# A stack copy moved to VectorE, register loads among the products, and w1 in smaller pieces

## The chip, the cores and the metric

The kernel runs on one core of one Trainium2 chip. The time is the device time of one execution in microseconds; with several executions it is their median. TensorE is called PE in the profile, VectorE DVE, ScalarE ACT, GpSimd POOL and SyncE SP.

## The reference

Two stages, one behind the other, in float32.

1. Local attention. Inputs `q`, `k`, `v` are 4 x 8 heads x 768 rows x 64. Each chunk of 32 rows attends to 8 memory rows, 16 rows on its left, its own 32 and 8 on its right, 64 columns in all: `softmax(q k^T / 8) v`.
2. A mixture of experts. The 3072 tokens of 512 numbers each choose one of 8 experts by the largest of 8 logits. An expert keeps up to `capacity` (768) tokens. It computes `relu(x w1) w2` with `w1` 512 x 1024 and `w2` 1024 x 512, and the result is weighted with the gate's probability and put back at the token's row; all other rows are zero.

How many tokens an expert has depends on the data, so the kernel reads the counts into registers and branches on them.

## The kernel before, in words

**Precision.** A product of two float32 matrices is made from three matmuls on split operands: each operand is a rounded part (`hi`) and the rest (`lo`), and `hi*hi + lo*hi + hi*lo` is summed in PSUM. So each weight matrix has to be split before use: ACT casts `hi` from the raw weights, and DVE or POOL subtracts to get `lo` (`split` for `w1`, `split2` for `w2`).

**Attention.** 24 tiles of 128 tokens, `t` = 0 to 23, run as a pipeline written out by hand: in step `t` come the scores of tile `t` (L502), the transposes of the tile before, the value product of the one before that (`value`, L539), the transposes of its output and the logits. SP loads `k` and `q` two segments ahead and `v` in blocks of two tiles. DVE copies the overlapping value rows (`copy_v`, L407, instructions of L417). Once a group of tiles has its logits, `route` gives small DVE operations, one at each `tick`, that compute expert and slot of each token; POOL then scatters the rows to DRAM (`put`, L799). In the steps of `W1_AT` SP also loads a quarter of expert 0's `w1` (L226), and in the steps of `PLAN` an eighth of it is split: the cast on ACT (L826), the subtraction on POOL (L827).

**Expert 0 ahead of the rest.** The first 256 rows of expert 0 (`EARLY`) are computed while the last tokens are still routed: `early` does their first layer, and `expert(0)` their second, in two products of 24 matmuls each, of 128 rows, `mm2` with t = 0 and 1. Each is read out by DVE as `y` (L959, `put_y`) and scattered by POOL (L960).

**An expert.** `layer1` computes the first layer for 512 columns in four pairs of blocks. The number of columns that are really computed is chosen by `If` on the count `m` (256, 320, 384 or 512, a branch of L893). ACT and DVE turn each block into `hhi` and `hlo` (`relu`, L875 and L876), and between the pairs the next expert's `w2` is split. Then come the tiles of the second layer, the last tile first (`last_tile`, L927): eight blocks of two matmuls, with the transposes of the next expert's rows in between, in fours. Where the last tile holds at most 64 rows, its `hhi` and `hlo` are laid side by side in one tile, so that the third matmul of each block can be left out. That copy is `stack` (L920): it copies 64 columns of `hlo` into the free columns of `hhi`, for blocks 0 to 5 behind the third pair and for blocks 6 and 7 behind the fourth. It is POOL's, under a `Switch` on bit 1 of `m + 1`.

**What sets the order.** Each engine runs its own list in the order of the program text, with semaphores between engines. So a late instruction on POOL holds whoever needs its result, and all that stands behind it on POOL. All loads of SP share the DMA engines with POOL's scatters and with the loading of instructions.

**Registers.** `values` (L793) loads numbers of an SBUF tile into the registers of an engine (TENSOR_LOAD in the trace): `m` for PE, DVE and POOL, `a` (from the tile `big`) for these and ACT. Before the change this is done in `experts`, ahead of expert 0's second layer. The banks `p2` are `lgp`, `b0` and the four of `p1`; `p1` are the banks of the first layer.

## Time and profile before

| what | value |
|---|---|
| median of 3 runs | 501.32 us (500.46 to 507.27) |
| the profiled execution | 505.29 us, of which the span is 503.5 us |
| PE, DVE, ACT, POOL busy | 463.4, 310.7, 232.0, 119.6 us |
| DMA, mean over the span | 157 GB/s, 79.26 MB |
| granted PE clock, mean | 0.986 |

The span reaches from the first to the last instruction. Busy time counts an engine's computing instructions. Matmuls are pipelined and their ends are modelled, so two matmuls in a row overlap in the rows, and the step from start to start is what one costs. In a timeline, what stands in brackets is the idle time of the engine ahead of the row, and what is held to have ended it.

### The profile page before, as it was taken

The page shows a single profiled execution, that of the slowest core. Times are in us where ns is not written, and L with a number is a line of the kernel's source. Part 1 is how long each engine was busy: PE and PEld are TensorE (multiplying, and loading weights), DVE is VectorE, ACT ScalarE, POOL GpSimd, SP SyncE. Part 2 cuts the span into 40 slices and gives each one's busy share as a digit, 9 for nine tenths or more (in the row PEclk, how much of TensorE's full clock was granted, in tenths as well). Part 3 has the DMA queues.
Part 4 walks back from the last instruction along what each step waited for, and adds up shares of the span by engine and source line. Part 5 has one row for each costly group of instructions (what it writes and reads, how often), then busy time and mean ns, then how long its engine had stood idle before and what let it go on. Part 6 is the DMA issues. An engine that isn't in the chain of part 4 may idle for free. (4 is left out here: it accounts for less than half of the span.)

```text
span 503.5 us, 12006 instructions
## 1 busy us (share of the span) xinstructions
PE 463.4 (92%) x4317; PEld 390.1 (77%) x4317; DVE 310.7 (62%) x676; ACT 232.0 (46%) x415; POOL 119.6 (24%) x160
## 2 busy tenths in 40 slices
PE   7899989898889985998999999999999999799993
PEld 6778877676678784887777899889988988677782
DVE  5989798998767642556645635745552685575310
ACT  6588768688442321525434415624430563443300
POOL 7621133556535341020200210010022011010011
PEclk9899999999999998899999999999999999999998
DMA  8687698987674666036470472534501644540011
GB/s 210 140 211 164 164 251 230 239 216 203 173 252 180 172 261 213 5 105 214 173 259 12 169 272 76 189 122 161 171 29 49 236 170 159 180 153 29 3 40 42
DMA packets 79393, 79.26 MB, mean 157 GB/s; under 512 B 33330, under 2 KB 60078, under 8 KB 79216
## 3 DMA queue, kind: packets, MB, share of 16 engines
q1 hardware_dynamic: 74416, 62.33, 43.3%
q0 software_dynamic: 4800, 14.95, 7.8%
q8 instruction: 65, 1.06, 0.9%
q14 instruction: 112, 0.92, 0.6%
HBM read 61.25 MB, written 15.99 MB: 153 GB/s over the span
## 5 line engine op out<-in xcount | busy, mean ns | idle before, releaser
L875 ACT ACTIVATE hhi<-ps 128x512 fp32r<-128x512 f32 x68 | 40.7, 599 | 148.8 <-PE ps L862 136.7
L876 DVE SCALAR_TENSOR_TENSOR hlo<-ps,hhi 128x512 fp32r<-128x512 f32 x68 | 47.0, 691 | 72.5 <-ACT hhi L875 69.7
L960 POOL DMA_INDIRECT out_dram<-y,tok x28 | 31.8, 1137 | 196.6 <-DVE y L959 73.6
L953 PE MATMUL ps<-w2hi,hhi 128*128 128x512 f32 x160 | 64.1, 401 | 1.4 <-DVE hlo L344 1.4
L862 PE MATMUL ps<-xhi,w1hi 128*128 128x320 f32 (+3 forms) x288 | 59.4, 328 | 5.9 <-DVE hlo L876 2.2
L953 PE MATMUL ps<-w2lo,hhi 128*128 128x512 f32 x160 | 62.9, 393 | 0.0
L953 PE MATMUL ps<-w2hi,hlo 128*128 128x512 f32 x160 | 62.5, 391 | 0.0
L862 PE MATMUL ps<-xhi,w1lo 128*128 128x320 f32 (+3 forms) x288 | 57.7, 322 | 0.0
L862 PE MATMUL ps<-xlo,w1hi 128*128 128x320 f32 (+3 forms) x288 | 57.6, 322 | 0.0
L862 PEld LDWEIGHTS ps<-xhi,w1hi 128*128 128x128 f32 x288 | 45.2, 188 | 10.4 <-ACT w2hi L853 3.7
L862 PEld LDWEIGHTS ps<-xhi,w1lo 128*128 128x128 f32 x288 | 45.9, 188 | 3.0
L862 PEld LDWEIGHTS ps<-xlo,w1hi 128*128 128x128 f32 x288 | 45.9, 188 | 2.8
L959 DVE TENSOR_SCALAR y<-ps,xg 128x512 f32<-128x512 f32 x20 | 15.0, 750 | 49.8 <-PE ps L953 45.0
L854 DVE TENSOR_TENSOR w2lo<-raw,w2hi 128x512 fp32r<-128x512 f32 x64 | 42.5, 705 | 0.0
L843 DVE TENSOR_TENSOR xlo<-ps,xhi 128x512 fp32r<-128x512 f32 x34 | 23.4, 690 | 27.2 <-ACT xhi L842 26.6
L827 DVE TENSOR_TENSOR w1lo<-raw,w1hi 128x512 fp32r<-128x512 f32 x56 | 36.6, 684 | 2.6 <-DVEq L846 0.6
L842 ACT CAST xhi<-ps 128x512 fp32r<-128x512 f32 x34 | 19.9, 587 | 38.8 <-PE ps L838 32.0
L953 PEld LDWEIGHTS ps<-w2hi,hhi 128*128 128x128 f32 x160 | 30.0, 188 | 8.6 <-DVE hlo L344 1.6
L853 ACT CAST w2hi<-raw 128x512 fp32r<-128x512 f32 x64 | 36.3, 620 | 0.0
L552 PE MATMUL ps<-vw,pT 128*32 128x130 f32 x768 | 29.2, 277 | 7.3 <-issue 3.7
L826 ACT CAST w1hi<-raw 128x512 fp32r<-128x512 f32 x64 | 35.5, 620 | 0.8
L953 PEld LDWEIGHTS ps<-w2hi,hlo 128*128 128x128 f32 x160 | 30.1, 188 | 7.0
(163 smaller groups left out, 810.3 us busy)
## 6 DMA issues: line engine op xcount, KB each, us to landing
raw<-in_moe_w_dram SPq DMA_DIRECT2D x15, 2048.0 KB
raw<-in_q_dram SPq DMA_DIRECT2D x11, 512.0 KB
raw<-in_k_dram SPq DMA_DIRECT2D x10, 512.0 KB
vw<-in_v_dram SPq DMA_DIRECT2D x49, 64.0 KB
xg<-x_d SPq DMA_DIRECT2D x3, 792.0 KB
vw<-in_v_dram SPq DMA_DIRECT2D x31, 72.0 KB
xg<-x_d SPq DMA_DIRECT2D x4, 528.0 KB
xg<-x_d SPq DMA_DIRECT2D x2, 1056.0 KB
```

The costliest lines, as they stand in the source:

```text
L552: nc.tensor.matmul(ps[32 * c4:32 * c4 + 32, i * 130:i * 130 + 130], pT[:, pr * P + 32 * c4:pr * P + 32 * c4 + 32], vw[:, c + c4 + 1, :, pr ...
L826: self.nc.scalar.copy(out=hi[sl], in_=raw[sl])
L827: (eng or self.nc.vector).tensor_tensor(out=lo[sl], in0=raw[sl], in1=hi[sl].bitcast(F32), op=ALU.subtract)
L842: nc.scalar.copy(out=self.xhi[:, d:d + k, sl], in_=pv)
L843: nc.vector.tensor_tensor(out=self.xlo[:, d:d + k, sl], in0=pv, in1=self.xhi[:, d:d + k, sl].bitcast(F32), op=ALU.subtract)
L853: self.nc.scalar.copy(out=self.w2a[:, j], in_=self.raw2[:, j])
L854: self.nc.vector.tensor_tensor(out=self.w2b[j // 4][:, j % 4], in0=self.raw2[:, j], in1=self.w2a[:, j].bitcast(F32), op=ALU.subtract)
L862: self.nc.tensor.matmul(ps, a[:, d, fs], b[:, d, o:o + w], start=(i + d == 0), stop=(i == 2 and d == KD - 1))
L875: self.nc.scalar.activation(out=self.hhi[hs], in_=ps, func=AF.Relu)
L876: self.nc.vector.scalar_tensor_tensor(out=self.hlo[hs], in0=ps, scalar=0.0, in1=self.hhi[hs].bitcast(F32), op0=ALU.max, op1=ALU.subtract)
L953: self.nc.tensor.matmul(ps, a[:, f, t * P:t * P + P], b, start=(f == 0 and i == 0), stop=(f == KF - 1 and i == 2))
L960: nc.gpsimd.indirect_dma_start(out=self.out[:, :], out_offset=bass.IndirectOffsetOnAxis(ap=tok[:, t:t + 1], axis=0), in_=y, in_offset=None ...
```

## The change

Three edits.

1. `stack` runs on DVE, under an `If` of DVE alone on a register `mv` that only DVE loads; and it stands directly behind the relu, ahead of the two `split2` of its pair.
2. The loads of `m` and `a` move out of `experts` into `expert(0)`: `m` (and DVE's `mv`) between the two early products, `a` within the second. The two products go to `p2[0]` (`lgp`) and `p2[1]` (`b0`); before they went to `p2[1]` (`b0`) and `p2[2]` (the first bank of `p1`). The second product's `y` is made ahead of the transposes of the third and fourth quarter.
3. Expert 0's `w1` is loaded in eight parts of 256 KB in the steps 3, 5, ..., 17 (before: four of 512 KB in 11, 13, 15, 17) and split in sixteen parts of 128x256 in the steps 6 to 21 (before: eight of 128x512 in 14 to 21).

```diff
-W1_AT = (11, 13, 15, 17)
-PLAN = ((14, 6), (15, 6), (16, 6), (17, 6), (18, 6), (19, 6), (20, 6), (21, 6))
+W1_LOAD, W1_SPLIT = range(3, 19, 2), range(6, 22)
...
-            if t in W1_AT:
-                k = W1_AT.index(t)
-                nc.sync.dma_start(out=self.raw1[:, k, :], in_=self.w1[0, k * P:(k + 1) * P, :])
-            split1(t)
+            if t in W1_LOAD:
+                _, d, f = w1_part(W1_LOAD.index(t), len(W1_LOAD))
+                nc.sync.dma_start(out=self.raw1[:, d, f], in_=self.w1[0, d * P:(d + 1) * P, f])
+            if t in W1_SPLIT:
+                self.split(self.raw1, self.w1hi, self.w1lo, w1_part(W1_SPLIT.index(t), len(W1_SPLIT)), nc.gpsimd)
...
-        self.m = self.values(self.m32, ENGS, 4 * nt + 1)
-        self.a = self.values(self.big, ENGS + (ET.Activation,), 2)
...
+            if g >= KF - 4:
+                self.stack(e, slice(0, g + 2) if g == KF - 4 else slice(g, g + 2))
             for _ in fs:
                 if todo2:
                     self.split2(todo2)
-            if g >= KF - 4:
-                self.stack(e, slice(0, g + 2) if g == KF - 4 else slice(g, g + 2))
...
-        for n in self.tc.Switch({ET.Pool: ((self.m[e] + 1) >> 1) & 1}, 2):
-            if n:
-                self.nc.gpsimd.tensor_copy(out=self.hhi[:, fs, o + P // 2:o + P], in_=self.hlo[:, fs, o:o + P // 2])
+        with self.tc.If((self.mv[e] + 1) & 2):
+            self.nc.vector.tensor_copy(out=self.hhi[:, fs, o + P // 2:o + P], in_=self.hlo[:, fs, o:o + P // 2])
...
-            for t in range(TA - 1):
-                self.layer2(e, t, tok)
-            ps = self.p2[self.order.index(TA - 1)]
-            for i, fs in enumerate((range(0, 3), range(3, 6), range(6, KF))):
-                self.mm2(ps, TA - 1, fs)
-                self.trans_x(e, i, 1)
-            self.put_y(e, ps, TA - 1, tok)
-            self.trans_x(e, KD - 1, 1)
+            self.mm2(self.p2[0], 0, range(KF))
+            self.m = self.values(self.m32, ENGS, 4 * self.nt + 1)
+            self.mv = self.values(self.m32, ET.DVE, 4 * self.nt + 1)
+            self.put_y(e, self.p2[0], 0, tok)
+            self.mm2(self.p2[1], 1, range(0, 3))
+            self.trans_x(e, 0, 1)
+            self.mm2(self.p2[1], 1, range(3, 6))
+            self.trans_x(e, 1, 1)
+            self.a = self.values(self.big, ENGS + (ET.Activation,), 2)
+            self.mm2(self.p2[1], 1, range(6, KF))
+            self.put_y(e, self.p2[1], 1, tok)
+            for d in range(2, KD):
+                self.trans_x(e, d, 1)
```

**The stack copy in expert 0.** On POOL, before, behind the third pair of blocks (L1048 and L923 are the `Switch`: the register arithmetic, the computed branch and its hints):

```order
L1048 SWITCH_STRIDE
L1048 ISA
L1048 REGISTER_ALU
L1048 ISA x2
L923 BRANCH_PREFETCH_HINT
L1048 UNCONDITIONAL_BRANCH
L923 BRANCH_PREFETCH_HINT
L925 COPY hhi<-hlo 128x6x64
```

On DVE, now, at the same place (L872 are the two relus of the pair, L919 the `If`):

```order
L872 SCALAR_TENSOR_TENSOR hlo<-ps,hhi 128x512 x2
L919 REGISTER_ALU x2
L919 COMPARE_AND_BRANCH
L920 COPY hhi<-hlo 128x6x64
L919 UNCONDITIONAL_BRANCH x2
```

The copy has left POOL and stands between the relus of one pair and the branches of the next; in the other experts the two `w2` subtractions follow it.

**The first early product on PE.** Before (L342 ends the early first layer):

```order
L342 MATMUL ps<-xlo,w1hi 128x256 x8
L795 TENSOR_LOAD m_77
L795 TENSOR_LOAD big
L953 MATMUL ps<-w2hi,hhi 128x512
L953 MATMUL ps<-w2lo_2753,hhi 128x512
```

Now the first product (into `lgp`) follows L340, the former L342, at once, and the load of `m` stands at its end:

```order
L948 MATMUL lgp<-w2hi,hhi 128x512
L948 MATMUL lgp<-w2lo_3042,hhi 128x512
L948 MATMUL lgp<-w2hi,hlo 128x512
L791 TENSOR_LOAD m_77
L948 MATMUL ps<-w2hi,hhi 128x512
L948 MATMUL ps<-w2lo_2773,hhi 128x512
```

The loads no longer stand ahead of the first product; `big` is loaded after the second group of four transposes, inside the second product.

## Rows read from the trace of the kernel before

**Rows 1.** The page, part 1: busy time of each engine (share of the span) and instructions.

```profile
PE 463.4 (92%) x4317; PEld 390.1 (77%) x4317; DVE 310.7 (62%) x676; ACT 232.0 (46%) x415; POOL 119.6 (24%) x160
```

**Rows 2.** PE's waits: line, what it waited for, us in total, times, longest us.

```profile
PE lgp L932 <- POOL hhi L925: 6.2, 1, 6.2
...
PE ps L862 <- DVE w2lo L854: 2.0, 1, 2.0
```

**Rows 3.** Windows of 2 us in expert 0: window, its length, busy us (and instructions) of PE, PEld, DVE, ACT and POOL, granted clock, DMA share, GB/s.

```profile
194.00:196.00 2.00, 0.39 (x3) 0.19 (x2) 0.86 (x2) 0.60 (x1) 0.00 (x0) 1.00 1.02 359
196.00:198.00 2.00, 0.00 (x0) 0.00 (x0) 0.00 (x0) 0.00 (x0) 0.00 (x0) 1.00 1.02 379
198.00:200.00 2.00, 0.00 (x0) 0.00 (x0) 0.00 (x0) 0.00 (x0) 0.00 (x0) 0.72 0.28 111
200.00:202.00 2.00, 1.36 (x3) 1.16 (x4) 0.00 (x0) 0.00 (x0) 0.51 (x1) 0.50 0.01 4
```

**Rows 4.** Timeline at the last tile of expert 0: start, us, engine, line, operation, idle time ahead.

```profile
194.06 0.33 PE L871 MATMUL ps<-pad 128*64 128x64 f32 x2
...
200.08 0.51 POOL L925 CAST hhi<-hlo 128x384 fp32r<-128x384 f32 x1 [6.23 <-DMA raw<-in_moe_w_dram]
...
200.64 0.79 PE L932 MATMUL lgp<-w2hi,hhi 128*128 128x512 f32 x1 [6.25 <-POOL hhi L925]
...
205.74 0.48 PE L932 MATMUL lgp<-w2hi,hhi 128*128 128x512 f32 x1
```

**Rows 5.** The same place in expert 1, where the copy is not needed.

```profile
235.49 0.50 PE L932 MATMUL lgp<-w2hi,hhi 128*128 128x512 f32 x1
...
238.25 0.49 PE L932 MATMUL lgp<-w2hi,hhi 128*128 128x512 f32 x1
```

**Rows 6.** Sequencers: single instructions of the `Switch` on POOL in the window from 194 to 200 us (duration ns min/median/max, first and last start), and the branches of the width helper L893 on DVE and on PE over the whole span.

```profile
L1048 POOLq COMPARE_BRANCH  x1: 43/43/43, 194.5 to 194.5; - x1
...
L923 POOLq BRANCH_PREFETCH_HINT  x1: 43/43/43, 199.8 to 199.8; - x1
...
L893 PEldq COMPARE_BRANCH  x92: 64/207/3489, 176.9 to 463.7; - x92
L893 DVEq COMPARE_BRANCH  x92: 41/56/69, 180.3 to 469.1; - x92
```

**Rows 7.** Register loads of `values` on PE's sequencer, same columns.

```profile
L795 PEldq TENSOR_LOAD <-m x1: 781/781/781, 162.0 to 162.0; - x1
L795 PEldq TENSOR_LOAD <-big x1: 600/600/600, 162.9 to 162.9; - x1
```

**Rows 8.** Timeline at the first early product.

```profile
161.86 1.11 PE L342 MATMUL ps<-xlo,w1hi 128*128 128x256 f32 x8
...
164.33 0.50 PE L953 MATMUL ps<-w2hi,hhi 128*128 128x512 f32 x1 [1.36 <-DVE hlo L344]
...
166.06 2.48 DVE L854 TENSOR_TENSOR w2lo<-raw,w2hi 128x512 fp32r<-128x512 f32 x4
```

**Rows 9.** Timeline at the start of expert 0's first layer.

```profile
178.28 0.74 DVE L959 TENSOR_SCALAR y<-ps,xg 128x512 f32<-128x512 f32 x1
178.89 0.59 ACT L842 CAST xhi<-ps 128x512 fp32r<-128x512 f32 x1 [1.25 <-PE ps L871]
...
179.17 0.82 PE L862 MATMUL ps<-xhi,w1hi 128*128 128x320 f32 x4 [1.46 <-DVE y L959]
```

**Rows 10.** POOL's and DVE's timelines in the attention stage.

```profile
89.29 1.28 POOL L827 TENSOR_TENSOR w1lo<-raw,w1hi 128x512 fp32r<-128x512 f32 x1 [3.29 <-ACT w1hi L826]
...
93.72 1.27 POOL L827 TENSOR_TENSOR w1lo<-raw,w1hi 128x512 fp32r<-128x512 f32 x1 [1.64 <-ACT w1hi L826]
...
89.14 0.16 DVE L700 SCALAR_TENSOR_TENSOR r_slot<-r_idx,r_pos 128x4 f32<-128x4 f32 x1
89.33 1.25 DVE L703 SCALAR_TENSOR_TENSOR r_dst<-r_ov,r_slot 128x4 int32<-128x4 f32 x1
...
93.77 1.76 DVE L417 COPY vw<-vw 24x768 f32<-24x768 f32 x1
```

**Rows 11.** Scores of the tiles 3, 14 and 22 on DVE (the row maximum, one for each tile).

```profile
28.38 0.67 DVE L519 TENSOR_REDUCE m<-ps 128x8 f32<-128x512 f32 x1
...
84.16 0.68 DVE L519 TENSOR_REDUCE m<-ps 128x8 f32<-128x512 f32 x1
...
132.43 0.68 DVE L519 TENSOR_REDUCE m<-ps 128x8 f32<-128x512 f32 x1
```

**Rows 12.** Groups of instructions by shape: line, engine, operation, tiles, shape, count, busy us, mean ns of one.

```profile
L826 ACT CAST w1hi<-raw 128x512 fp32r<-128x512 f32 x64 | 35.5, 620 | 0.8
...
L925 POOL CAST hhi<-hlo 128x384 fp32r<-128x384 f32 x5 | 3.2, 632 | 59.3 <-ACT w2hi L853 53.1 <-DMA raw<-in_moe_w_dram 6.2
...
L925 POOL CAST hhi<-hlo 128x128 fp32r<-128x128 f32 x5 | 1.8, 355 | 23.2 <-PE ps L838 9.8 <-ACTq L912 5.0 <-DVE xlo L843 4.9
...
L325 ACT CAST xhi<-ps 128x256 fp32r<-128x256 f32 x4 | 1.2, 387 | 1.4 <-DMA raw<-in_moe_w_dram 1.4
...
L498 DVE COPY kw<-kw 64x672 f32<-64x672 f32 x9 | 4.6, 506 | 1.4 <-ACT kw L481 1.3
```

**Rows 13.** A window of 10 us in the attention stage (columns as in rows 3), and SP's loads of `w1` (duration of the issue, ns min/median/max).

```profile
30.00:40.00 10.00, 9.24 (x186) 7.55 (x185) 9.39 (x26) 8.22 (x14) 3.96 (x9) 1.00 1.01 230
...
L226 SPq DMA_DIRECT2D raw<-in_moe_w_dram x4: 449/542/1525, 78.3 to 114.2; - x4
```

More of the change, by code (lines that the diff above doesn't have):

```diff
@@ L184, in attention, with w1_part @@
         ends = {t0 + w - 1: g for g, (t0, w) in enumerate(GROUPS)}
-        todo = [(k, slice(f, f + F // 2)) for k in range(KD) for f in (0, F // 2)]
-        def split1(t):
-            if any(i == t for i, _ in PLAN):
-                self.split(self.raw1, self.w1hi, self.w1lo, (slice(None), *todo.pop(0)), nc.gpsimd)
+        def w1_part(i, n):
+            w = KD * F // n
+            return slice(None), i * w // F, slice(i * w % F, i * w % F + w)
         for t in range(NTL):
@@ L975, in expert @@
         tc, nc = self.tc, self.nc
-        m, a = self.m[e], self.a[e]
         todo1 = list(range(KF)) if e + 1 < E else []
@@ L994, in expert @@
             nc.sync.dma_start(out=self.raw2, in_=self.w2[e + 1].rearrange("(k p) d -> p k d", p=P))
+        m, a = self.m[e], self.a[e]
         def split1(n):
```

## The prediction

> **What bounds the kernel now.** I read the page first, then PE's waits, then the windows and timelines around the longest of them. TensorE is busy for 463.4 of the 503.5 us [rows 1], so the kernel is bound by it and what can be won is mostly its idle time. The reader is to see in the list of PE's waits that one wait alone holds 6.2 us: L932, the first matmul of the last tile, behind POOL's `hhi` copy of L925, once [rows 2]; two shorter ones (1.4 and 1.5 us) stand at the start of the early second-layer product and of the first layer [rows 8, 9]. The windows show what the long one costs beyond itself: from 196 to 200 us PE does nothing, and the granted clock is 0.72 from 198 and 0.50 from 200 [rows 3].
>
> The timeline of that place [rows 4]: PE issues its last small matmul at 194.06 (0.33 long), and starts L932 at 200.64, 0.05 us after POOL's copy (200.08 + 0.51) ended. The copy itself is short. What is late is POOL's sequencer: it does the branch of the `Switch` at 194.5 and its next instruction, a hint of L923, comes at 199.8 [rows 6]. In between nothing is recorded on POOL, the DMA engines are full (share 1.02) until 198 to 200, when a 2 MB load of weights ends, and only then does POOL go on [rows 3]. So I read this as the fetch of the jump's target waiting behind that load, and not as a wait for data.
>
> The attention stage before 133 us has VectorE and TensorE near their limits together. There a subtraction of `w1` on POOL (L827, 1.28 us) holds up VectorE: the same kind of small routing operation that takes 0.16 us at 89.14 takes 1.25 at 89.33, beside a POOL piece that began at 89.29; a copy of L417 takes 1.76 at 93.77 beside the piece of 93.72 [rows 10].
>
> **The change, part by part.** *The stack copy goes to VectorE.* In expert 0 the copy of six blocks then stands right behind the relu on VectorE and is done while PE still computes the last pair of blocks; the branch around it is VectorE's own kind, of which 92 took 41 to 69 ns [rows 6]. The idle time of 6.25 us [rows 4] goes but for about 0.25 (the usual gap of a branch): **-6.0**. The cold clock goes with it: from the first L932 matmul at 200.64 to the ninth at 205.74 it is 5.10 us, and the same eight matmuls and eight transposes in expert 1 take from 235.49 to 238.25, 2.76 us [rows 4, 5]: **-2.3**. The ends: 0, if another wait of the same length is behind it, and -8.6. I take -8.3, because PE's own operands and the next expert's rows are needed in expert 1 too and make no wait there.
> In the other seven experts PE waited for no POOL copy [rows 2], so nothing is won. What VectorE gains in work: a copy of 128x384 has no row there; the nearest are 64x672 between two places of SBUF, 0.51 us, above, and a routing operation of 0.16, below; POOL takes 0.63 and 0.36 for the two sizes [rows 10, 12]. Five stacked experts, two copies of some 0.35 and 0.25, sixteen branches of 0.06: 4 us on an engine that is busy for 62% of the span [rows 1]. What hides it is that in both pairs the copy comes ahead of two `w2` splits that nobody waits for at once, and that the last tile needs the second copy only for its seventh block, after twelve matmuls and twelve transposes, some 4 us by [rows 5]. Without that cover it is +4. I take 0.
> What is queued behind the copy on VectorE: those splits, the next relu and the transposes' `xlo`. POOL loses its sixteen jumps; its output scatters come earlier, and nobody waits for them.
>
> *Register loads and banks.* Before the first product TensorE's sequencer loads `m` and `big`, 0.78 and 0.60 us [rows 7]; the matmul at 164.33 then also waits for the relu of a bank that the early phase used: 1.36 us of idle time [rows 8]. Now the product goes to `lgp`, free since the counts, and can start at about 163. But the halves of `w2` are late next: VectorE's last four L854 begin at 166.06 and end at 168.54 [rows 8]; at 0.233 us a matmul the product would need the fifth half at 166.0, gets it at 166.75, and ends at 169.3; started at 164.33, it ends at 169.9. So **-0.6**, between 0 and -1.36. The loads move between matmuls; the one at 162.0 began while matmuls until 162.97 were still to run [rows 7, 8], so the queue ahead covers 0.78; if it doesn't, +0.8 and +0.6. I take 0. VectorE's second load of `m` (some 0.8) lies where it waits for PE.
> At 179.17 the first layer waits 1.46 us for `y`, which frees its bank [rows 9]. With `y` in another bank PE waits for `xhi` of the last quarter, which ACT starts at 178.89 and ends 0.59 later. If that stays, only 0.1 us is won; if it moves up behind the cast before it, 1.3. I take the middle, **-0.7**.
>
> *w1 in smaller pieces.* Bytes and subtracted elements are the same. ACT does sixteen casts in place of eight; a half one costs 0.39 in place of 0.62 by the nearest row [rows 12], so +1.3 us on ACT, which waits for others in this stage. SP issues four more loads, 0.54 us each in the median, behind value loads and ahead of the next `k` and `q` loads, at tiles 3 to 17 and no longer 11 to 17 [rows 13]: hidden while the loads run two segments ahead; if not, 2.2 us. Half of the 2 MB goes into the stretch of tiles 3 to 9, where the DMA share is already 1.01 in one window [rows 13]; 1 MB at the 230 GB/s of that window is 4.5 us if nothing covers it. Against it: tiles 3 to 14 took 55.8 us for 11, or 5.1 each, tiles 14 to 22 took 48.3 for 8, or 6.0 each [rows 11]; the eight pieces of POOL lie in the latter. Some 6 us of these are VectorE held up (in the two rows shown 1.1 each, and eight pieces). A half piece holds it 0.64 at most: sixteen by 0.35 to 0.45 are 5.6 to 7.2, some of them in early tiles where VectorE waits for loads anyway. The bounds are -4 (all in idle time) and +6 (1 MB of loads and the issues on the path). I take **-1**, nearest to the rows on VectorE.
>
> **Sum.** -8.3 - 0.6 - 0.7 - 1.0 = -10.6. The profiled execution took 505.29, so 494.7. Its own time is 4.0 above the median of the runs, 501.32; the same step from the median gives 490.7. The trace can't say whether the 4.0 us are in the stall that goes (then the median gains less). I take the middle: **493**.
>
> A rule of the Trainium skill, "Runtime: NRT & Kernel Launch", section Instruction fetch mechanics, speaks against branches as such: a taken branch whose target is outside the small window that the sequencer holds has to wait for a DMA fetch. By it every one of the sixteen new branches on VectorE may stall as POOL's did; POOL's 5.3 us agree with it; VectorE's 92 branches show no such case. What the sum would be by it is the time of the first rival.
>
> **Rivals.**
> 1. *VectorE's new branches stall as POOL's jump does*; this is the case that ends slower. Place: the two branches of each expert after the relu. TensorE's own branches of the same helper reach 3.49 us where VectorE's stay under 0.07 [rows 6]; of one of them 2.0 us stayed visible as a wait of PE [rows 2]. One such stall per expert: 8 x 2.0 = +16, so 509. It decides once a branch takes longer than the splits behind which it hides, about 1.3 us. Against it: VectorE's branches skip a handful of instructions, PE's skip whole products.
> 2. *The stall is not in a typical run, or another wait replaces it.* For it: the 4.0 us between profile and median, and that the end of the stall hangs on when a load was issued. Then only the three smaller terms and some of the clock remain: 497 to 501, say 499.
> 3. *The early loads cost.* The attention stage is paced by loads in tiles 3 to 9: +6 in place of -1, 500.
> 4. *The stage gains more*, since short pieces slip between VectorE's operations: -4 to -6 in place of -1, 488.
>
> **Chances.** Forecast 0.60 (489 to 497), rival 1 0.05, rival 2 0.17, rival 3 0.08, rival 4 0.10. 2% of 501.32 is 10.0 us, about what a measurement of this kernel can tell from no change: faster by that is below 491.3, which holds rival 4 and four tenths of the forecast, 0.34; slower is above 511.3, the upper part of rival 1, 0.03; the rest 0.63. A range of 487 to 500.5 leaves out rival 1, the late part of rivals 2 and 3, and the best of rival 4.
>
> **What will show it.** In the new profile: no wait of PE at L927 (the last tile there) and a clock of 1.0 around 195 to 200 us; the copy on VectorE under 0.5 us and its branches under 0.1; PE's gaps at about 163 and 178 under 0.5; the half pieces on POOL near 0.65 and VectorE's longest L417 copies shorter; tiles 14 to 22 at 5.5 us each and tiles 3 to 14 at no more than 5.3. Wrong if PE stands as long for something else in expert 0, or if the first value product of tiles 3 to 9 waits for loads.

## The result, and the profile after

The changed kernel takes 486.17 us (median of 4 runs, 483.69 to 486.98); the kernel before, run beside it, 500.89. The ratio is 0.967, with a 95% interval of 0.958 to 0.976: faster by 14.7 us. The forecast was 493, and its range began at 487.0, so the time lies 0.8 us below it. The sign was right and the size too small, by about 7 us. In the runs below, ratios leave out a few executions that the record marks as slow, among them one of f_after of 738.03 us at a granted clock of 0.561, while a median is that of all executions unless the text says otherwise.

The profiled execution of the changed kernel took 483.69 us, its span is 481.8. The page's part 1 shows that the same 4317 matmuls fill a larger share of a shorter span [rows 1]:

```profile
PE 458.3 (95%) x4317; PEld 386.9 (80%) x4317; DVE 308.9 (64%) x686; ACT 232.6 (48%) x423; POOL 118.2 (25%) x158
```

TensorE's waits behind the attention stage (line, waited for, us in total, times, longest): nothing waits for POOL any more [rows 2], and the longest wait of this stage, 1.7 us, ends with one of TensorE's own branches (L908, 3.63 us on its sequencer, until 214.0).

```profile
PE ps L867 <- issue: 3.0, 3, 1.7
PE ps L858 <- ACT w2hi L849: 1.7, 1, 1.7
```

The windows around the last tile of expert 0 (columns as in [rows 3]) have no hole and a clock of 1.00:

```profile
176.00:178.00 2.00, 2.00 (x16) 2.00 (x15) 0.93 (x2) 0.60 (x1) 0.00 (x0) 1.00 0.24 87
178.00:180.00 2.00, 2.00 (x15) 2.00 (x15) 1.29 (x3) 0.60 (x1) 0.99 (x1) 1.00 0.37 86
180.00:182.00 2.00, 2.00 (x13) 1.52 (x12) 0.90 (x3) 0.60 (x1) 0.00 (x0) 1.00 0.82 178
```

In the timeline there, VectorE's copy (0.36 us) follows the relu at once, and the last tile (L927) begins 0.26 us after the small matmul of L867; before, these were 6.6 us apart [rows 4]. The copy of the last two blocks comes at 181.87 and takes 0.23 us.

```profile
177.63 0.69 DVE L872 SCALAR_TENSOR_TENSOR hlo<-ps,hhi 128x512 fp32r<-128x512 f32 x1 [1.07 <-ACT hhi L871]
...
178.35 0.36 DVE L920 CAST hhi<-hlo 128x384 fp32r<-128x384 f32 x1
...
180.41 0.33 PE L867 MATMUL ps<-pad 128*64 128x64 f32 x2
...
180.67 0.50 PE L927 MATMUL lgp<-w2hi,hhi 128*128 128x512 f32 x1
...
181.87 0.23 DVE L920 CAST hhi<-hlo 128x128 fp32r<-128x128 f32 x1
```

The `If` around it, on VectorE's sequencer (ns min/median/max):

```profile
L919 DVEq COMPARE_BRANCH  x26: 43/47/63, 177.8 to 451.8; - x26
```

The two gaps of TensorE at the early products [rows 8, 9] are gone as well: the first product (L948 into `lgp`) and the first layer (L858) follow what stands ahead of them.

```profile
151.33 1.11 PE L340 MATMUL ps<-xlo,w1hi 128*128 128x256 f32 x8
152.28 0.40 PE L948 MATMUL lgp<-w2hi,hhi 128*128 128x512 f32 x1
...
165.21 0.33 PE L867 MATMUL ps<-pad 128*64 128x64 f32 x2
165.47 0.95 PE L858 MATMUL ps<-xhi,w1hi 128*128 128x320 f32 x4
```

The scores of tile 14 and of tile 23 on VectorE, as in [rows 11], now lie 44.1 us apart:

```profile
84.86 0.68 DVE L517 TENSOR_REDUCE m<-ps 128x8 f32<-128x512 f32 x1
...
128.99 0.69 DVE L517 TENSOR_REDUCE m<-ps 128x8 f32<-128x512 f32 x1
```

In the kernel before, the first profile has 55.6 us for these nine tiles, from 84.16 [rows 11] to the scores of tile 23:

```profile
139.72 0.69 DVE L519 TENSOR_REDUCE m<-ps 128x8 f32<-128x512 f32 x1
```

This looked like a gain of 11 us of the attention stage. The next section shows that it isn't.

### The profile page after: what moved, and what is told of

Its sections match the earlier page's. It is cut to its first block, busy times and chain, and to the rows that moved or that the text cites. A ratio compares the mean times of both kernels' runs of the same rounds, so it can differ in the third digit from the quotient of the medians.

```text
span 481.8 us, 11847 instructions
## 1 busy us (share of the span) xinstructions
PE 458.3 (95%) x4317; PEld 386.9 (80%) x4317; DVE 308.9 (64%) x686; ACT 232.6 (48%) x423; POOL 118.2 (25%) x158
## 4 chain that ended last, share of the span: by engine, by line
PE 52%; DMA 18%; issue 13%; DVE 10%; ACT 2%; SPq 1%; POOLq 1%; DVEq 0%; ACTq 0%
PE ps L858 19%; DMA out_dram<-y,tok 13%; PE ps L948 13%; PE lgp L927 5%; DMA raw<-in_q_dram 3%; PE ps L834 2%; PE ps L550 2%; DVE vw L415 2%; PE ps L463 2%; PE ps L509 2%; PE ps L331 2%; ACT kw L479 1%; DVE m L517 1%; DVE d L520 1%; SPq L397 1%
## 5 line engine op out<-in xcount | busy, mean ns | idle before, releaser
L872 DVE SCALAR_TENSOR_TENSOR hlo<-ps,hhi 128x512 fp32r<-128x512 f32 x68 | 47.0, 691 | 68.6 <-ACT hhi L871 65.7
L858 PE MATMUL ps<-xhi,w1hi 128*128 128x320 f32 (+3 forms) x288 | 59.5, 328 | 3.6 <-ACT w2hi L849 1.7
L948 PE MATMUL ps<-w2hi,hhi 128*128 128x512 f32 x152 | 60.9, 401 | 0.0
L948 PE MATMUL ps<-w2lo,hhi 128*128 128x512 f32 x152 | 59.8, 393 | 0.0
L948 PE MATMUL ps<-w2hi,hlo 128*128 128x512 f32 x152 | 59.4, 391 | 0.0
L858 PE MATMUL ps<-xhi,w1lo 128*128 128x320 f32 (+3 forms) x288 | 57.7, 322 | 0.0
L858 PE MATMUL ps<-xlo,w1hi 128*128 128x320 f32 (+3 forms) x288 | 57.7, 322 | 0.0
L858 PEld LDWEIGHTS ps<-xhi,w1hi 128*128 128x128 f32 x288 | 45.2, 188 | 8.3 <-issue 2.1
L858 PEld LDWEIGHTS ps<-xhi,w1lo 128*128 128x128 f32 x288 | 45.9, 188 | 2.9
L858 PEld LDWEIGHTS ps<-xlo,w1hi 128*128 128x128 f32 x288 | 45.9, 188 | 2.8
L850 DVE TENSOR_TENSOR w2lo<-raw,w2hi 128x512 fp32r<-128x512 f32 x64 | 41.2, 685 | 0.9 <-DVEq L919 0.6
L822 ACT CAST w1hi<-raw 128x512 fp32r<-128x512 f32 (+1 forms) x72 | 37.1, 573 | 0.9
L948 PEld LDWEIGHTS ps<-w2hi,hlo 128*128 128x128 f32 x152 | 28.6, 188 | 6.7
L948 PEld LDWEIGHTS ps<-w2hi,hhi 128*128 128x128 f32 x152 | 28.5, 188 | 6.7
L948 PEld LDWEIGHTS ps<-w2lo,hhi 128*128 128x128 f32 x152 | 28.5, 188 | 5.8
```

The source lines that it names most:

```text
L822: self.nc.scalar.copy(out=hi[sl], in_=raw[sl])
L850: self.nc.vector.tensor_tensor(out=self.w2b[j // 4][:, j % 4], in0=self.raw2[:, j], in1=self.w2a[:, j].bitcast(F32), op=ALU.subtract)
L858: self.nc.tensor.matmul(ps, a[:, d, fs], b[:, d, o:o + w], start=(i + d == 0), stop=(i == 2 and d == KD - 1))
L872: self.nc.vector.scalar_tensor_tensor(out=self.hlo[hs], in0=ps, scalar=0.0, in1=self.hhi[hs].bitcast(F32), op0=ALU.max, op1=ALU.subtract)
L948: self.nc.tensor.matmul(ps, a[:, f, t * P:t * P + P], b, start=(f == 0 and i == 0), stop=(f == KF - 1 and i == 2))
```

## The experiments

Theory A, after the result: the three parts add up, and w1 was sized too small. Rival B: the stack copy was sized too small. First each part by itself, and the kernel before once more. The diffs shown are cut to the lines that matter. Wherever the copy is on VectorE, `mv` is loaded and the copy stands ahead of the two splits, as in the change; the place alone was not tried.

**stack_only.**

```diff
-        for n in self.tc.Switch({ET.Pool: ((self.m[e] + 1) >> 1) & 1}, 2):
-            if n:
-                self.nc.gpsimd.tensor_copy(...)
+        with self.tc.If((self.mv[e] + 1) & 2):
+            self.nc.vector.tensor_copy(...)
```

> The stack copy alone on VectorE; registers, banks and w1 as before. Theory A (the gain is the sum of three separate parts, and w1 in smaller pieces is the one that was sized too small): about -8, 493 us, ratio 0.984; in the trace the last tile of expert 0 starts within 0.5 us of the last small matmul and the granted clock stays at 1.0 there; tile 23's scores come as late as in the kernel before. Rival B (the stack copy was sized too small, because the stall of POOL's jump is longer in a typical run than in the one profiled, and w1 is worth about the -1 of the prediction): about -12, 489 us, ratio 0.976.

Measured: 489.15 us, ratio 0.976 (0.972 to 0.981), or 11.8 us of 501.51. That is rival B's number. The stack copy alone brings about four fifths of the change.

**w1_only.**

```diff
-W1_AT = (11, 13, 15, 17)
-PLAN = ((14, 6), (15, 6), ..., (21, 6))
+W1_LOAD, W1_SPLIT = range(3, 19, 2), range(6, 22)
```

> Only w1's loads (eight of 256 KB) and splits (sixteen of 128x256) as in the change; the stack copy on POOL and registers and banks as before. Theory A: -4 to -6, 495 to 497 us, ratio 0.988 to 0.992; tiles 3 to 14 take 1 to 2 us longer and tiles 14 to 23 come 5 to 11 us sooner; POOL's jump in expert 0 still holds TensorE for 4 us or more. Rival B: -1, 500 us, ratio 0.998, and tile 23 at 136 us or later. Rival C (the stop of VectorE and TensorE from 135 to 139.5 us is an accident of the one profile): the late tiles gain 5 to 7 us instead of 11 by the profile, and the time is in between.

Measured: 499.61 us, ratio 0.9995 (0.996 to 1.003): nothing that can be told from zero, as rival B says. Its late tiles (14 to 23) do come sooner, 44.0 us, with tile 23 at 130.8 and not at 136 or later as rival B had it; but TensorE waits 11.0 us for POOL's copy.

**regs_only.**

```diff
-        self.m = self.values(self.m32, ENGS, 4 * nt + 1)
-        self.a = self.values(self.big, ENGS + (ET.Activation,), 2)
...
+            self.mm2(self.p2[0], 0, range(KF))
+            self.m = self.values(self.m32, ENGS, 4 * self.nt + 1)
+            self.put_y(e, self.p2[0], 0, tok)
...
+            self.a = self.values(self.big, ENGS + (ET.Activation,), 2)
```

> Only the register loads and the banks of the two early products as in the change. Theory A: TensorE's gaps of 1.36 us ahead of the first early product and of 1.46 us ahead of the first layer fall under 0.3 each; -2 to -3, 498 to 499 us, ratio 0.994 to 0.996. Rival (the POOL jump comes behind a load that is issued as much earlier, or the w2 halves are late): less than 1 us is left of it at the end, ratio 0.998 or more.

Measured: 501.98 us, ratio 1.001 (0.997 to 1.005). The gaps ahead of the first product and of the first layer are not in its profile, and yet the time is no shorter, as its rival said.

**before_again**, without an edit.

> The kernel before, unchanged, for a second profile. Theory A with rival C's point: the wait of TensorE for POOL's copy in expert 0 is there again, 5 to 7 us long. If the stop of VectorE and TensorE between 135 and 139.5 us belongs to the kernel, it is there again with 3 us or more, and the time is about 505; if it is an accident of the first profile, tile 23's scores come at about 135 us and the time is about 501.

Measured: 496.73 us. The scores of tiles 14 and 23 in this second profile:

```profile
83.03 0.68 DVE L519 TENSOR_REDUCE m<-ps 128x8 f32<-128x512 f32 x1
...
131.76 0.69 DVE L519 TENSOR_REDUCE m<-ps 128x8 f32<-128x512 f32 x1
```

So the same kernel needs 48.7 us for these tiles, not 55.6. Of all ten profiles of kernels without the w1 edit, eight lie between 47.5 and 48.7. The first profile had three long steps that these eight have not: 7.95 us from tile 15 to 16 (in the eight: 5.8 to 6.3), 6.6 from 20 to 21 (4.3) and 7.3 from 22 to 23 (about 3). The wait for POOL's copy is there again, 7.0 us.

So theory A falls and B's numbers stand, but why should the copy be worth 11.8 where the profile showed 6.2 and a cold clock of 2.3? The profile of regs_only answers: its wait is 12.0 us. In the list of TensorE's waits:

```profile
PE lgp L930 <- POOL hhi L923: 12.0, 1, 12.0
```

In its timeline, SP's load of expert 1's `w2`, POOL's two output scatters and the copy:

```profile
182.50 0.38 SPq L995 DMA_DIRECT2D raw<-in_moe_w_dram  x1
...
182.66 0.97 POOL L958 DMA_INDIRECT out_dram<-y,tok  x1 [8.35 <-DVE hlo L874]
...
191.21 0.97 POOL L958 DMA_INDIRECT out_dram<-y,tok  x1 [7.58 <-DMA out_dram<-y,tok]
195.78 0.51 POOL L923 CAST hhi<-hlo 128x384 fp32r<-128x384 f32 x1 [3.60 <-issue]
```

And the longest semaphore on POOL's sequencer at the scatters' line (ns min/median/max, first and last start):

```profile
L958 POOLq EVENT_SEMAPHORE  x1: 7290/7290/7290, 183.2 to 183.2; - x1
```

The reader is to see three starts: the load at 182.50, the first scatter at 182.66, the second not before 191.21. The second scatter writes the same output and waits for the first one's transfer (7.58 us, `DMA out_dram<-y,tok`; on the sequencer one semaphore of 7290 ns). Where a trace holds the moment at which the first one landed (five of the sixteen profiles), the second starts 0.76 to 0.78 us behind it, as 183.09 and 183.85 in before_again and 194.13 and 194.90 in late_scatter, below. The DMA engines are full until the second scatter starts (columns as in [rows 3]; the last three numbers are the granted clock, the DMA share and GB/s):

```profile
188.00:190.00 2.00, 0.00 (x0) 0.00 (x0) 0.00 (x0) 0.00 (x0) 0.00 (x0) 0.50 1.04 410
190.00:192.00 2.00, 0.00 (x0) 0.00 (x0) 0.00 (x0) 0.00 (x0) 0.79 (x1) 0.50 0.56 215
...
194.00:196.00 2.00, 0.00 (x0) 0.00 (x0) 0.00 (x0) 0.00 (x0) 0.22 (x1) 0.50 0.00 0
```

The packets of the two DMA queues (packets, MB, share of 16 engines), first from 183.6 to 187.6 us and then from 187.6 to 190.2; q1 carries the load and q0 POOL's scatter:

```profile
q1 hardware_dynamic: 459, 0.94, 93.2%
...
q1 hardware_dynamic: 389, 0.80, 78.9%
q0 software_dynamic: 80, 0.26, 24.8%
```

The scatter was issued at 182.66, and no packet of it runs in the first stretch: its first one comes at 187.97, 5.3 us after the issue, and then its packets share the engines with the load's. Only behind the second scatter follow the jump of the `Switch` and the copy. In the kernel before the same semaphore is there, but shorter; this was in its trace from the start. The two scatters and the load in its timeline:

```profile
188.66 0.97 POOL L960 DMA_INDIRECT out_dram<-y,tok  x1 [6.94 <-DVEq L912]
...
189.71 0.38 SPq L994 DMA_DIRECT2D raw<-in_moe_w_dram  x1
...
192.88 0.97 POOL L960 DMA_INDIRECT out_dram<-y,tok  x1 [3.25 <-DVE hlo L876]
```

The semaphores at L960 (ns min/median/max), the longest of which is the second scatter's:

```profile
L960 POOLq EVENT_SEMAPHORE  x3: 17/43/3633, 185.6 to 188.5; - x3
```

There the first scatter was issued 1.05 us **ahead** of the load, and the second waited 3.6 us. It is a race between two queues that nothing orders, and it decides between two sizes of the stall. That it goes both ways in one and the same program is seen in the profiles of the change and of stack_only, each of which was taken twice: the second scatter comes 9.6 us behind the first in after and 4.0 in f_after, 9.1 in stack_only and 4.0 in f_stack. In all sixteen profiles the order decides. Where the scatter is issued behind the load (nine), its first packet comes 4.6 to 5.6 us after its issue and the next scatter 8.0 to 9.6 after it; where it is issued ahead of the load or without it (seven), 1.55 and 3.8 to 4.2. Theory D: POOL is late for two reasons, the scatter that waits for a transfer and the jump that waits for its instructions; in the short kind the jump meets the 2 MB load, in the long kind the scatter does, and holds up all behind it.

**raw2_late** was to take the load away.

```diff
-        if e + 1 < E:
+        if 0 < e < E - 1:
             nc.sync.dma_start(out=self.raw2, ...)
...
         self.last_tile(e, tok, between)
+        if not e:
+            nc.sync.dma_start(out=self.raw2, ...)
```

> The kernel before, with one load moved: w2 of expert 1 (2 MB) is loaded behind expert 0's last tile and no longer behind its first layer. Theory D (POOL's copy is late because POOL's second output scatter waits for the first one's transfer and POOL's jump for its instructions, both through DMA engines that this load fills): both come while the DMA engines are idle; POOL's jump takes 2.6 to 3 us in place of 5.3, TensorE waits 3.5 to 5 us for the copy in place of 6 to 12, and the time is 494 to 498. Rival E (the jump is slow by itself, whatever the DMA engines do): the wait stays at 6 to 12 us and the time at 501.

Measured: 497.56 us, ratio 0.996 (0.992 to 1.001), and a wait of 5.6 us. It tells nothing: SyncE has nothing to do in the last tile, and issued the load at 181.68, as before. A line moved in the text is no transfer moved in time, if no instruction of that queue stands between.

**load_after** gives the load to ScalarE's queue, behind its casts of the last tile.

```diff
+        if not e:
+            nc.scalar.dma_start(out=self.raw2, ...)
```

> The kernel before, where w2 of expert 1 (2 MB) is loaded from ScalarE's queue, behind its casts in expert 0's last tile, so that it can't start before TensorE has passed the copy. (In raw2_late SyncE had nothing in between and issued the load as early as before, 181.68 us, so that run told nothing of the load.) Theory D: both waits on POOL meet idle DMA engines: the second scatter waits 3.3 us for the first and never 7 to 9, the jump takes 2.6 to 3 us in place of 5.3; TensorE waits 3 to 4.5 us for the copy in place of 6 to 12, and the time is 493 to 497, a ratio of 0.988 to 0.995. Rival E (the jump is slow by itself): 5.3 us for it, a wait of 6 us or more, 499 to 501.

Measured: 494.47 us, ratio 0.989 (0.983 to 0.995), as theory D said. The load starts at 197.09, long behind the copy. POOL's scatters and copy in the timeline:

```profile
181.25 0.97 POOL L960 DMA_INDIRECT out_dram<-y,tok  x1 [7.50 <-DVE hlo L876]
185.01 0.97 POOL L960 DMA_INDIRECT out_dram<-y,tok  x1 [2.78 <-DVE hlo L876]
189.44 0.51 POOL L925 CAST hhi<-hlo 128x384 fp32r<-128x384 f32 x1 [3.46 <-issue]
```

On POOL's sequencer, the second scatter's semaphore and the two ends of the jump (its branch, and the first instruction behind it):

```profile
L960 POOLq EVENT_SEMAPHORE  x1: 3164/3164/3164, 181.1 to 181.1; - x1
...
L1050 POOLq COMPARE_BRANCH  x1: 43/43/43, 186.6 to 186.6; - x1
...
L923 POOLq BRANCH_PREFETCH_HINT  x1: 43/43/43, 189.1 to 189.1; - x1
```

The semaphore is 3.2 us and the jump takes 2.5 (186.6 to 189.1), where it took 5.3 behind the load [rows 6] and 5.6 in before_again. TensorE still waits 4.9 (3 to 4.5 were expected): what is left is the jump and the scatter's own time. So the jump is slow by itself, and twice as slow behind the load. The time fell by 5.6 us (0.989 of the kernel before), and the wait is only some 1.4 below the mean of the three short ones (5.6 to 7.0): this suggests that the kernel before often waits longer than its profiles show.

**pool_if** leaves the copy on POOL and takes the jump away.

```diff
-        for n in self.tc.Switch({ET.Pool: ((self.m[e] + 1) >> 1) & 1}, 2):
-            if n:
-                self.nc.gpsimd.tensor_copy(...)
+        with self.tc.If((self.mp[e] + 1) & 2):
+            self.nc.gpsimd.tensor_copy(...)
```

> The kernel before, with POOL's Switch (a computed jump) replaced by an If on a register that POOL alone loads; the copy stays on POOL, at its old place. Theory D: the fetch of the jump goes, the wait of the second scatter for the first stays. Where the first scatter is issued ahead of the load, the copy comes 5 us earlier and TensorE waits about 1 us; where it is issued behind it, POOL stands 7 to 9 us in the scatter's wait and TensorE waits 7 to 9 us. In the mean 492 to 497. Rival F (the jump is the whole cause, as the prediction had it): as fast as with VectorE, 489 to 490, and no wait over 1.5 us. Rival E2 (POOL's branches fetch as slowly as its jump): 501.

Measured: 491.50 us, ratio 0.981 (0.976 to 0.986). In POOL's timeline the copy comes 1.7 us after the second scatter:

```profile
183.50 0.97 POOL L960 DMA_INDIRECT out_dram<-y,tok  x1 [3.09 <-DVE hlo L877]
185.19 0.51 POOL L925 CAST hhi<-hlo 128x384 fp32r<-128x384 f32 x1 [0.73 <-issue]
186.24 0.29 POOL L925 CAST hhi<-hlo 128x128 fp32r<-128x128 f32 x1 [0.54 <-DVEq L913]
```

In the page's part 3, the queue of instruction fetches (packets, MB, share):

```profile
q14 instruction: 65, 0.53, 0.3%
```

The same line of the kernel before:

```profile
q14 instruction: 112, 0.92, 0.6%
```

Without the sixteen jumps 47 packets of instructions fewer are fetched. The median of all four lies between the theories (492 to 497 and 489 to 490), and the three executions that the ratio takes, 487.01, 489.29 and 493.71, have a mean of 490.0, which is rival F's number. The one profile is of the short kind, where both expect about what it shows. So this run doesn't tell D from F, and a wait of 7 to 9 us for the second scatter without the jump was not caught.

**late_scatter** forces the order: twelve memsets of a scratch tile on POOL ahead of the first scatter, in the kernel before. **late_scatter_dve** is the change with the same memsets.

```diff
+        if not e and not t:
+            dl = self.my.tile([P, 128], F32, name="dl")
+            for _ in range(12):
+                nc.gpsimd.memset(dl, 0.0)
         nc.gpsimd.indirect_dma_start(out=self.out[:, :], ...)
```

> The kernel before, with twelve memsets of a scratch tile on POOL (some 2.4 us) ahead of the first output scatter of expert 0, so that it is issued behind the load of w2 in every execution. Theory D: the second scatter then waits 7 to 9 us for the first one's transfer, TensorE waits 11 to 13 us for POOL's copy in the profile, and the median lies 2 to 5 us above that of the kernel before, 502 to 506, a ratio of 1.004 to 1.010. Rival J (the order of scatter and load does not matter; POOL is late for another reason): the wait grows by no more than the 2.4 us of the memsets over the 6 to 7 us of the short kind, or the ratio is 1.002 or less.

Measured: 501.19 us, ratio 1.004 (1.000 to 1.008): the ratio is at the lower end of theory D's, its interval holds rival J's 1.002 too, and the median is below D's 502 to 506. The wait, 10.5 us, is above the 9.4 that rival J allows; but the memsets took 3.09 us and not 2.4, and with that J allows 10.1. What decides is the place of the wait. The timeline shows the long kind, with POOL's memsets, SP's load, the scatters and the copy:

```profile
182.56 3.09 POOL L963 MEMSET dl<- 128x128 f32 x12 [3.83 <-ACTq L912]
...
185.61 0.38 SPq L998 DMA_DIRECT2D raw<-in_moe_w_dram  x1
...
186.35 0.97 POOL L964 DMA_INDIRECT out_dram<-y,tok  x1 [0.70 <-issue]
...
194.90 0.97 POOL L964 DMA_INDIRECT out_dram<-y,tok  x1 [7.57 <-issue]
199.48 0.51 POOL L925 CAST hhi<-hlo 128x384 fp32r<-128x384 f32 x1 [3.61 <-issue]
```

The first scatter is 0.74 us behind the load and the second 8.55 behind the first, where the kernel before has 4.2, and rival J has no reason for that. The wait was expected to be 11 to 13. The median rises by only 1.6 us, as it would if many executions of the kernel before were of the long kind already; no profile of that kernel shows it.

> The change with the same twelve memsets at the same place. Theory D: the second scatter waits 7 to 9 us here too, but no copy stands behind it, so the time is that of the change, 486 to 488, and TensorE has no wait over 1 us in expert 0. Rival K (the order costs something by itself, by contention or by late output): 2 us or more above the change.

Measured: 485.04 us, ratio 0.972 (0.966 to 0.978). The second scatter again comes 8.05 us behind the first (180.68 and 188.73), but no copy stands behind it, and TensorE starts the last tile 0.26 us after the small matmul. The order costs nothing that can be seen by itself.

All profiles of expert 0 with the copy on POOL together (us; the start of each, and TensorE's wait):

| kernel | first scatter | load of `w2` | second scatter | copy | wait |
|---|---|---|---|---|---|
| before | 188.66 | 189.71 | 192.88 | 200.08 | 6.2 |
| before_again | 179.94 | 181.23 | 183.85 | 191.34 | 7.0 |
| raw2_late | 180.25 | 181.68 | 184.19 | 191.52 | 5.6 |
| regs_only | 182.66 | 182.50 | 191.21 | 195.78 | 12.0 |
| w1_only | 181.38 | 181.19 | 190.84 | 195.47 | 11.0 |
| no_stack | 177.87 | 177.85 | 187.34 | 191.90 | 11.9 |
| late_scatter | 186.35 | 185.61 | 194.90 | 199.48 | 10.5 |
| load_after | 181.25 | 197.09 | 185.01 | 189.44 | 4.9 |
| pool_if | 179.43 | 180.99 | 183.50 | 185.19 | 0.7 |

The mean wait of the first six, where nothing forces the order, is 9.0 us. From the start of the last tile to the end they take 303.2 us in the mean, and six profiles with the copy on VectorE (after, stack_only, stack_w1, stack_regs, f_stack, f_after) 301.2, or 301.0 with late_scatter_dve: the cold clock is some 2.0 us, if nothing else differs there. Together 11.0, against 11.8 measured for stack_only.

This mean needs care. The three short waits are all those of the kernel before and of raw2_late, whose load did not move; the three long ones are of kernels with an edit of w1 or of the registers. That the unchanged kernel too waits about 9 us in the mean is inferred from times, as estimates: 10.5 from load_after (its wait of 4.9 and the 5.6 it gained), 9.8 from stack_only (11.8 without the clock's 2.0), 8.2 from pool_if (9.5 gained and a wait of 0.7, less 2.0) and 8.4 from late_scatter (10.5 less the 2.1 of its ratio). By the intervals of the ratios the first two exclude the 6.3 of its own profiles, and the last two reach down to it.

**What the two other parts add.** stack_w1 is the change without the registers and banks, stack_regs the change without w1, no_stack the change with the copy back on POOL; f_stack and f_after are the copy alone and the change, on one chip.

> The change without its register loads and banks: stack copy on VectorE and w1 in smaller pieces. With the stall gone, what w1 gains early should reach the end: stack_only (489.15) minus 1 to 2, 487 to 488. Theory G (early gains were swallowed by the stall, whose end hangs on the load and the scatter, and show only once it is gone) says so; rival H (w1 is worth nothing in itself): 489 to 489.5.

Measured: 484.84 us, ratio 0.971 (0.967 to 0.974): below theory G's 487 to 488, and not rival H's 489.

> The change without the w1 edit: stack copy on VectorE, register loads and banks. Theory G: the 1.46 us gap ahead of the first layer goes and nothing takes it back, 489.15 minus 1.3 to 1.7, 487.5 to 488, and no gap over 0.3 us before expert 0's first layer. Rival H2 (the gap comes back as a wait of TensorE in expert 1): 489 to 489.5.

Measured: 487.29 us, ratio 0.977 (0.974 to 0.981), just below theory G's range. Its ratio is that of stack_only within the intervals, so that the registers and banks show in the trace (no gap ahead of the first layer) and not clearly in the time.

> The change with the stack copy put back on POOL under its Switch, behind the two w2 splits: register loads, banks and w1 as in the change. Theory G: what is gained ahead of the stall (about 3 us) only lets TensorE arrive sooner at it, and the first scatter then comes behind the load more often: TensorE waits 10 us or more for POOL, and the time is 498 to 502, a ratio of 0.995 to 1.003. Rival (the three parts simply add up): 500 less 3 for the two other parts, 496 to 497, ratio 0.993 or less.

Measured: 497.13 us, ratio 0.992 (0.988 to 0.997). That is the rival's number, not theory G's. Its profile does show the stall that G expected, 11.9 us: it is of the long kind, and 4.9 us longer than in before_again, while TensorE was 4.2 us earlier at the first layer (165.43 for 169.66). So in this one execution the early gain is swallowed. But the ten times of the kernel lie lower than the kernel before's by 3.4 us, so it isn't the rule. Whether w1 and the banks count fully ahead of the stall stays open: w1_only and regs_only say no, no_stack says yes, and their intervals overlap.

> The stack copy alone on VectorE, once more, on the same chip as f_after, to measure what the two other parts add behind it. Expected 0.976 of the kernel before, 488 to 489.5.

Measured: 490.00 us, ratio 0.979 (0.973 to 0.986).

> The change itself, on the same chip as f_stack. If the two other parts are worth what the traces show once the stall is gone (1.5 us for banks and registers, 1 to 3 for w1), it takes 2.5 to 4.5 us less than f_stack; if they are worth nothing, the same within 1 us.

Measured: 487.97 us, ratio 0.975 (0.968 to 0.982). Over the comparable executions, four of f_stack and three of f_after, the medians are 488.04 and 485.71. So the two other parts are worth 2.3 us here and 3.0 by the first runs of the two kernels (489.15 and 486.17); neither of the two expected cases is clearly hit, and the intervals overlap. stack_w1 is the fastest median of all, but not apart from the change.

## Why the prediction was wrong

**What bounds the kernel**, right. TensorE fills the span, and its one long wait was the place. The reading of the jump held: 5.3 us behind a load against 2.5 with idle DMA engines.

**The stack copy**, the step that failed: "-6.0" for the idle time. In its place the runs show 9.0 us in the mean of six profiles, in two kinds, 5.6 to 7.0 and 11.0 to 12.0, and 8.2 to 10.5 by the estimates from times. Two profiles of the kernel before show the short kind (6.2 and 7.0), so that its own share of the long kind is inferred and not seen. The prediction read the stall as the jump alone and took one execution for the typical one. What it overlooked was in the same trace: POOL's second scatter waits for the first one's transfer, and the first was issued only 1.05 us ahead of the load that was blamed for the jump. Had this been read, the long kind would have been a bound of the term: the transfer of the first scatter until the end of the load, some 4 to 5 us more than the 3.6 seen. The cold clock was right, some 2.0 for 2.3. So were the copies (0.36 and 0.23 us for "some 0.35 and 0.25"), VectorE's branches (at most 63 ns) and, all but a trace, the cover behind the splits: in expert 0 TensorE has no wait there. Late in the kernel (410.94 us) it waits 1.7 us behind one of its own branches, as it did before (2.0 us at 432.10 [rows 2]); in five of the other profiles with the copy on VectorE a wait of 1.8 to 2.0 us at this place is put down to the copy, which ends up to 0.3 us behind that branch.

**From where the sum was counted**, the second half of the miss. The prediction saw that the profiled execution took 4.0 us more than the median and asked whether that was in the stall; it took the middle, 493. It was not: that execution had a stall of the short kind, and long steps in the attention stage: tiles 3 to 23 took 111.3 us in it and 104.2 in before_again. Counted from the median the prediction's own steps gave 490.7, and with 11.0 for the stall and the clock instead of 8.3, 488.0. The change took 486.17 and, in f_after, 487.97.

**Registers and banks.** The gap of 1.36 us ahead of the first early product belongs to the first profile only; in before_again and the others the product follows at once, so "-0.6" was worth nothing. The gap of 1.46 ahead of the first layer is in every profile without this edit and in none with it: from the first early product to the first layer 14.84 us (before) and 14.72 (before_again), now 13.19. "-0.7" was 1.5 in the trace, since `xhi` on ScalarE no longer holds the first layer; in the times it is not clear (regs_only 1.001, and stack_w1 without it no slower than the change). The register loads cost nothing visible, as said.

**w1.** Net "-1.0" by two effects that were both larger. The late tiles (14 to 23) take 44.0 to 44.1 us in all six profiles with the edit, and 47.5 to 48.7 in eight without it (the two with long steps left out). The early tiles (3 to 14) take 56.2 to 59.1 against 54.7 to 57.1. Over both it is 101.6 against 103.8 in the mean: -2.2. On the whole a half piece holds VectorE less than the "0.35 to 0.45" that was allowed for. If each VectorE instruction beside a piece is compared with the median of its kind with nothing on POOL beside it, the excess comes to 6.5 to 7.0 us for the eight pieces (the "some 6" of the prediction) and to 3.4 to 4.1 for the sixteen, 0.2 to 0.26 each. In POOL's timeline of the changed kernel one piece:

```profile
89.37 0.72 POOL L823 TENSOR_TENSOR w1lo<-raw,w1hi 128x256 fp32r<-128x256 f32 x1 [2.89 <-ACT w1hi L822]
```

In VectorE's, the routing operation that it holds (0.16 us unhindered [rows 10]):

```profile
89.43 0.68 DVE L698 SCALAR_TENSOR_TENSOR r_slot<-r_idx,r_pos 128x4 f32<-128x4 f32 x1
```

All sixteen pieces (ns min/median/max):

```profile
L823 POOL TENSOR_TENSOR w1lo<-raw,w1hi x16: 719/740/987, 48.2 to 124.2; 128x256 fp32r<-128x256 f32 x16
```

That is 0.5 us where a whole piece cost 1.1 [rows 10], and more than the mean of a half piece; the half piece itself is longer than "near 0.65".

**The rivals.** Rival 1 did not happen. The rule of the Trainium skill that stands beside it ("Runtime: NRT & Kernel Launch", section Instruction fetch mechanics: a taken branch out of the window waits for a fetch) agrees with POOL's jump, which takes 2.5 us even with idle DMA engines. It does not show in an `If` around one copy: 43 to 63 ns on VectorE here, and pool_if has 65 packets of instructions where the kernel before has 112. Rival 2 has it the wrong way round: the stall was there in every profile with the `Switch`, and longer in half of those in which nothing forced the order. Rival 3 (early loads cost) was to act in tiles 3 to 9, and these are only 0.4 us longer in the mean; tiles 9 to 14, where half pieces run now (from 48.2 us on) and no piece ran before (the first at 89.3), are 1.3 longer. The early tiles lose 1.7 us together, the late ones gain 3.9, and that loads are the cause is not shown. Rival 4 gave nearly the right time, 488, for a wrong reason: the attention stage gained 2.2 us and not 4 to 6, and the rest is the stall.

## What to carry to other kernels

Where a long wait ends on an engine's queue, list everything that this queue did between its last useful instruction and the late one, semaphores included, and ask of each what would make it longer; two issues on different queues a microsecond apart are a race, and the profile shows one outcome of it. Take a second profile of the unchanged kernel, where there can be one, before a stage is compared by its traces: one execution had some 7 us of longer steps that a second one of the same kernel did not have. A small conditional copy on the critical path belongs on the engine that makes its input, and behind an `If`, not a computed jump.

## What was unexpected of the hardware

- A 256 KB scatter issued 0.0 to 0.7 us behind a 2 MB load is done only when the load nearly is (its last packet at 189.98 in regs_only, the load's at 191.74): the next scatter comes 8.5 to 9.6 us after it, against 3.8 to 4.2 where it was issued ahead of the load or without it. The Trainium skill says in "DMA: Bandwidth & Descriptors", section Queues, rings and completion order, that a DMA engine takes turns between its queues, a packet at a time. By it the scatter would share the engines with the load and, as an estimate from 256 KB more at the 410 GB/s of the window above, wait 0.6 us longer. It waited more than 4 us longer, so here the measurement decides. The turns themselves are in the trace: in regs_only 243 packets of the load run among the scatter's 64. From first to last packet the scatter takes 2.0 to 2.9 us beside the load and 1.0 to 1.2 without it; the larger part, 3.1 to 4.0 us, lies ahead of its first packet. Why that one comes so late stays open.
- A jump of `Switch` on POOL takes 2.5 us with idle DMA engines (load_after) and 5.3 to 5.6 behind a load, and sixteen of them go with 47 packets of instructions; with an `If` around the same copy the trace shows no such wait.
- Open: in two of ten profiles without the w1 edit, and in none of six with it, the attention stage has steps that are 2 to 4 us longer than in the others. In part the first profile shows why: from 93.77 to 98.01 VectorE's two large copies of L417 take 1.76 and 1.82 us beside POOL's work, and 0.67 and 0.68 in before_again. From 135 to 139.4 TensorE runs its value products in small groups, with gaps for which the profile names nothing. Whether the edit has to do with it can't be told from these numbers.
